# The first weight loads in order of use, another order of the first batch's Newton steps and M, idle products in slots 0 to 2

## The chip, the cores and the metric

One core of a Trainium2 chip runs the whole program. It has TensorE (PE, with its weight loads PEld), VectorE (DVE), ScalarE (ACT) and GpSimd (POOL) as engines that compute, SyncE (SP) as the queue that issues the transfers, and 16 DMA engines. The metric is the device time of one execution in microseconds. The inputs lie in the chip's memory, and all that is needed to prepare them counts.

## The reference

A Nyström attention with 32 landmarks, a six-step iteration for an inverse, and behind it two feed-forward networks:

```python
q_lm = q.reshape(B, H, 32, S // 32, D).mean(axis=3)      # B, H, S, D = 4, 8, 576, 64
k_lm = k.reshape(B, H, 32, S // 32, D).mean(axis=3)
A, Bm, C = sm(q, k_lm), sm(q_lm, k_lm), sm(q_lm, k)      # softmax of scaled scores
Z = Bm.T / (norm1(Bm) * norminf(Bm) + 1e-6)
for _ in range(6):
    Z = 2 * Z - Z @ Bm @ Z
x = heads_side_by_side(A @ Z @ C @ v)                    # 2304 x 512
h = x @ w_in;   x = (h * clip(h + 3, 0, 6) / 6) @ w_out  # 512 -> 2048 -> 512
h = x @ w_in2;  x = where(h > 0, h, exp(min(h, 0)) - 1) @ w_out2
```

The four weight matrices come as 64-bit floats and have to be converted on the chip; the tensors q, k and v are 32-bit.

## The kernel before

**Slots.** The first network runs in slots: a slot is one block of 128 of the 2048 hidden columns for half a batch (288 tokens). Its first products (`slot_a1`, lines 837 to 865: six products h<-atl/ath,nh/nl into a bank "h") multiply the attention's factors directly: n is M times the weight matrix (`attn_n`, 804 to 832), and at is the transposed softmax A (`attn_at`, 791 to 802). Then ACT and DVE form the activation (gf, g), and three slots later the second products (`slot_a2`, 867 to 886) add into four accumulators x. M itself (`finish`, 646 to 666) comes from the inverse Q and the values; Qd is Q spread over four heads, t0 the normalised values.

**The first part.** `start` (729 to 784) computes the first batch's attention up to the first slot. The order on PE, DVE, ACT and POOL is written out by hand in the string `PLAN` (723 to 727): each letter runs one step of a generator. b, c, a, v and B, C, A, V are the steps of the scores, the softmax of q and the values for the two head groups (a's and A's fifth step is the exponential on ACT, their sixth the sum, the reciprocal and a product on POOL); i is a step of `inverse` (586 to 644): three to set up, then for each of the six Newton iterations one step for PE's product and one for DVE's, and a last one that hands over Q; f is a step of `finish`; n makes the first 128 columns of n; t is `attn_at`, with three steps; x and y run the next conversion step of a weight unit on ACT or DVE; w is an idle product, 128x128 of the identity into a bank that nobody reads. PE works an idle product as two instructions, a product in 32-bit floats in general so.

**Weights.** A unit is one 128-column piece of a weight matrix, 512 KB of 64-bit floats. `steps` (211 to 241) loads it and then converts it with two passes on ACT, two on DVE and one addition on POOL. `units` holds four units of the first matrix (0 to 3), twelve of the second (l, l0 to l11), and four more of the first (m, m0 to m3). The digits, l and m in `PLAN` issue their loads. Slot by slot, `first_half` (1044 to 1088) converts one unit of each matrix, in the order 0, 1, 2, 3, then m0 with l0, m1 with l1 and so on. The tiles are named u, un or ub by their place.

**Queues.** All loads go through SP's queue. There the order isn't that of the program: the scheduler takes the instruction with the lowest `wanted` value first (`wanted`, 151). q and k have -70, unit 0 -66, v -65, unit 1 -64, the other eighteen all -50. On the four computing engines the program's order holds until slot 35 (`strict`); from slot 36 on the scheduler lays out their order, except where it is tied by hand. The second batch's attention is laced into slots 0 to 35 by the string `PLAN1` (1090); `newton` (675 to 715) does the third and fourth batch.

Of the kernel before, what the change touches and what calls it, by code (L numbers as in the profile page):

```python
# [10 lines left out]
F32 = mybir.dt.float32  # L11
# [20 lines left out]
def nystrom_ffn_kernel(ctx: ExitStack, tc, q, k, v, w_in1, w_out1, w_in2, w_out2, out):  # L32
# [32 lines left out]
    B, G, _, _, S = q.shape  # L65
# [58 lines left out]
    vec, act, pool, pe = InOrder(nc.vector), InOrder(nc.scalar), InOrder(nc.gpsimd), InOrder(nc.tensor)  # L124
# [15 lines left out]
    ident = const.tile([128, 128], F32, name="ident")  # L140
# [10 lines left out]
    def wanted(s):  # L151
        tc.cur_priority = int(1000 * (s + 100))
# [38 lines left out]
    banks, marks = {}, {}  # L191
# [51 lines left out]
    def run(gen):  # L243
        for _ in gen:
            pass
# [397 lines left out]
            yield 1.0  # L643
        return X[:, :, 2]

    def finish(b, Q, cvs, sc):

        t0 = ap_.tile([128, G, D], F32, name="t0", tag="t0")
        vec.scalar_tensor_tensor(
            out=sc[:, 0], in0=sc[:, 0], scalar=1e-9, in1=sc[:, 1], op0=ALU.add, op1=ALU.add  # L650
        )
        vec.reciprocal(out=sc[:, 0], in_=sc[:, 0])
        vec.tensor_tensor(out=t0, in0=cvs, in1=sc[:, 0].unsqueeze(2).to_broadcast([128, G, D]), op=ALU.mult)
        Qd = ap_.tile([128, G, 4, 32], F32, name="Qd", tag="Qd")
        vec.tensor_tensor(
            out=Qd, in0=Q.unsqueeze(2).to_broadcast([128, G, 4, 32]),
            in1=onesbd.rearrange("p (h j) -> p h j", h=4).unsqueeze(1).to_broadcast([128, G, 4, 32]), op=ALU.mult,
        )
        yield 1.0
        mps = bank()[:, 0:128]  # L660
        for g in range(G):
            amm(mps[64 * g:64 * g + 64, :], t0[:, g, :], Qd[:, g].rearrange("p h j -> p (h j)"), True, True)
        yield 0.5
        mt = ap_.tile([128, 4, 32], F32, name="mt", tag="mt", bufs=1)
        vec.tensor_copy(out=mt.rearrange("p a c -> p (a c)"), in_=mps)
        mt_t[b] = mt
# [8 lines left out]
    def newton(b):  # L675

        EB, sb, sc, cvs = newton_tiles()
        s = [SB * (b - 1) + (NEW if b > 1 else NEW1)]
        kept = {}

        def go(gen, n=99):
            for _ in range(n):
                wanted(s[0])
                try:
                    s[0] += next(gen) * (PACE if b > 1 else PACE1)
                except StopIteration:
                    return

        def keep(key, gen):
            kept[key] = yield from gen  # L690

        go(prep(b, 0))
        go(score_b(b, 0, sb, EB))
        go(keep(0, score_c(b, 0, sc)))
        go(soft(b, 0))
        go(values(b, 0, kept[0], cvs))
        go(prep(b, 1))
        go(score_b(b, 1, sb, EB))
        inv = keep("Q", inverse(EB, sb))
        sC = keep(1, score_c(b, 1, sc))  # L700
        sA = soft(b, 1)
        go(inv, 1)
        go(sC, 2)
        go(inv, 1)
        go(sC)
        go(inv, 2)
        go(sA, 3)
        go(inv, 2)
        v1 = values(b, 1, kept[1], cvs)
        go(v1, 2)  # L710
        go(inv, 2)
        go(sA)
        go(v1)
        go(inv)
        go(finish(b, kept["Q"], cvs, sc))

# [2 lines left out]


    PLAN = """
        0123llllmmmmllllllll kk b cc k bb k c B CC B c B c i i C xx v a i C v a C
        iwwavi iwwavVi vViwwAyVi aAiwwAVi VxxiwwAi aiwwyi
        ixAfwwwfwwwAfwwwtyywwwnwwwtwwxt
    """

    def start():

        EB, sb, sc, cvs = newton_tiles()
        kept = {}

        def keep(key, gen):
            kept[key] = yield from gen

        warm = bank()[:, 0:128]
        units = [[u, None] for u in conv_in1(0)]
        units += [[conv_out1(kk), None] for kk in range(NFILL)]
        units += [[u, None] for u in conv_in1(1)]  # L740

        def preps():
            for g in range(G):
                yield from prep(0, g)

        def fill(eng):

            for x in units:
                if x[1] and x[1][0] is eng:
                    x[1] = next(x[0], ())  # L750
                    while x[1] and x[1][0] is pool:
                        x[1] = next(x[0], ())
                    return

        make = {
            "k": preps, "f": lambda: finish(0, kept["Q"], cvs, sc), "n": lambda: attn_n(0, 0, 128),
            "i": lambda: keep("Q", inverse(EB, sb)), "t": lambda: attn_at(0, 0, vec),
        }
        for g in range(G):
            for name, gen in (  # L760
                ("b", lambda g=g: score_b(0, g, sb, EB)),
                ("c", lambda g=g: keep(g, score_c(0, g, sc))), ("a", lambda g=g: soft(0, g)),
                ("v", lambda g=g: values(0, g, kept[g], cvs)),
            ):
                make[name.upper() if g else name] = gen
        gens = {}
        for c in "".join(PLAN.split()):
            wanted(-60)
            if c in "xy":
                fill(act if c == "x" else vec)  # L770
            elif c == "w":
                pe.matmul(warm, lhsT=ident, rhs=ident, start=True, stop=True)
            elif c in "lm" or c.isdigit():
                wanted(-66 if c == "0" else -64 if c == "1" else -50)
                x = units[int(c)] if c.isdigit() else next(
                    x for x in (units[MPC:] if c == "l" else units[MPC + NFILL:]) if x[1] is None
                )
                x[1] = next(x[0], ())
            else:
                if c not in gens:  # L780
                    gens[c] = make[c]()
                next(gens[c], None)
        run(gens["t"])
        return units, gens["n"]
# [252 lines left out]
    def loads(b):  # L1037
        load_v(b, 0)
        for g in range(G):
            for what in "kq":  # L1040
                yield
                load_qk(b, g, what)

    def first_half(units, n0):

        outs = units[MPC:MPC + NFILL] + [[conv_out1(kk), None] for kk in range(NFILL, NKT)]
        groups = [units[0:2], units[2:4]]
        for j in range(NKT):
            group = [outs[j]]
            if MPC + j < NKT:  # L1050
                if j % MPC == 0:
                    ins = [[u, None] for u in conv_in1(j // MPC + 1)] if j else units[MPC + NFILL:]
                group.insert(0, ins[j % MPC])
            groups.append(group)
        ns, na = n0, 1
        sp.on = True
        for i in range(-PRE, NKT):
            between[0] = banks["h"].tile([128, 512], F32, name="h", tag="h")
            stream(groups, i + PRE + 1)
            wanted(i)  # L1060
            if i >= 0:
                run(slot_a1(i))
            while na < min(NKT, i + (NLEAD if 0 < i < MPC - 2 else 1) + 1):
                if na % MPC == 0:
                    run(ns)
                    ns = attn_n(0, na // MPC, 256)
                next(ns, None)
                na += 1 if na < MPC else 2
            if i >= DELAY:
                run(slot_a2(i - DELAY))  # L1070
            if i == NKT - 1:
                stream(groups, len(groups) + 3)
                between[0] = None
            if i < 0:
                continue
            if i >= GATE1:
                yield
        run(ns)
        for i in range(NKT, END):
            wanted(i)  # L1080
            a1, a2 = slot_a1(i), slot_a2(i - DELAY)
            next(a1)
            yield
            for dm in range(NDM):
                next(a1, None)
                next(a2, None)
                yield
            run(a2)

    PLAN1 = "ssssssuulslullslsssspppspsssppspppssssosssbbcsbsocsccscsaPasvaoavsssPvvosPavPasssPossPssPPssssssssBPoCCBssCCBososssisCsssisAississiAoAssissisVosiVAVVioiAsssAVisisisiioisssfftftssssotsnTssonssnosnsssnsnsTnosssnsssTssssssss"  # L1090

    def second_half(slots):

        EB, sb, sc, cvs = newton_tiles()
        kept = {}
# [4 lines left out]
        def parts():  # L1100
# [1 line left out]
                yield from attn_n(1, c, 256)  # L1102

        make = {
            "u": lambda: attn_at(0, 1), "o": splits, "l": lambda: loads(1), "f": lambda: finish(1, kept["Q"], cvs, sc), "n": parts,
            "i": lambda: keep("Q", inverse(EB, sb)), "t": lambda: attn_at(1, 0), "T": lambda: attn_at(1, 1),
        }
        for g in range(G):
# [6 lines left out]
        gens = {"s": slots}  # L1115
# [159 lines left out]
```

## Time and profile before

| what | value |
|---|---|
| median of 3 runs | 841.47 us (841.1 to 843.55) |
| the profiled execution's own time | 841.77 us |
| its span, first to last instruction | 840.0 us |
| PE busy | 795.5 us, 95% |
| PE weight loads busy | 697.0 us, 83% |
| DVE busy | 511.3 us, 61% |
| ACT busy | 445.7 us, 53% |
| POOL busy | 335.4 us, 40% |
| mean granted TensorE clock | 0.977 |
| moved by DMA | 165.63 MB |

Busy time is what the profiler records for one execution; a busy PE is not PE at its peak, since the ends of products are modelled. A row of the trace gives the start, the duration, the engine, the operation, what it writes and reads, how many instructions are merged in the row (x), and in brackets how long the engine was idle just before and what ended that. The idle time of an engine that isn't on the path to the end costs nothing. Nearly all instructions carry the line 110, that of the helper through which every one is issued, so they are told apart by their tiles.

### The profile page before, as it was taken

The page shows a single profiled execution, that of the slowest core. Times are in us where ns is not written, and L with a number is a line of the kernel's source. Part 1 is how long each engine was busy: PE and PEld are TensorE (multiplying, and loading weights), DVE is VectorE, ACT ScalarE, POOL GpSimd, SP SyncE. Part 2 cuts the span into 40 slices and gives each one's busy share as a digit, 9 for nine tenths or more (in the row PEclk, how much of TensorE's full clock was granted, in tenths as well). Part 3 has the DMA queues.
Part 4 walks back from the last instruction along what each step waited for, and adds up shares of the span by engine and source line. Part 5 has one row for each costly group of instructions (what it writes and reads, how often), then busy time and mean ns, then how long its engine had stood idle before and what let it go on. Part 6 is the DMA issues. An engine that isn't in the chain of part 4 may idle for free.

```text
span 840.0 us, 15410 instructions
## 1 busy us (share of the span) xinstructions
PE 795.5 (95%) x5650; PEld 697.0 (83%) x5650; DVE 511.3 (61%) x1026; ACT 445.7 (53%) x977; POOL 335.4 (40%) x348
## 2 busy tenths in 40 slices
PE   5669999999999999999999899999999999999998
PEld 4447778779888898979989789999989899999996
DVE  6488867647535565356585877656565545645544
ACT  3178654555646655576565565655544434534433
POOL 2256666636655545445656756431380000000000
PEclk9759999999999999999999999999999999999999
DMA  9935972386558433664482377586763564663531
GB/s 336 372 101 151 312 248 65 98 255 221 177 171 251 148 125 117 210 217 161 143 315 85 116 254 287 207 310 246 252 217 139 184 224 170 229 234 139 198 129 75
DMA packets 95563, 165.63 MB, mean 197 GB/s; under 512 B 7232, under 2 KB 51264, under 8 KB 95488
## 3 DMA queue, kind: packets, MB, share of 16 engines
q1 hardware_dynamic: 95488, 164.66, 57.9%
q8 instruction: 44, 0.72, 0.4%
q14 instruction: 31, 0.25, 0.1%
HBM read 119.54 MB, written 45.09 MB: 196 GB/s over the span
## 4 chain that ended last, share of the span: by engine, by line
PE 70%; DVE 6%; DMA 5%; POOL 3%; issue 3%; ACT 2%; SPq 1%; POOLq 0%; DVEq 0%; ACTq 0%
PE x L110 38%; PE h L110 27%; PE bk L110 4%; DVE u L110 2%; DMA u<-in_moe_w_in 1%; POOL x L110 1%; DMA w1c<-w1d 1%; DVE gf L110 1%; DMA u<-in_moe_w_out 1%; DVE gl L110 1%; DVE x L110 1%; ACT gf L110 1%; SPq L110 1%; POOL xf L110 1%; DMA x<-x1d 1%
## 5 line engine op out<-in xcount | busy, mean ns | idle before, releaser
L110 PE MATMUL h<-x,wi 128*128 128x384 f32 x1008 | 205.7, 339 | 0.8 <-DVE y L110 0.7
L110 PE MATMUL x<-gh,wo 128*128 128x288 f32 x896 | 201.4, 300 | 3.5 <-ACT xs L110 3.2
L110 PEld LDWEIGHTS h<-x,wi 128*128 128x128 f32 x1008 | 182.0, 189 | 15.2 <-DVE u L110 1.3
L110 PEld LDWEIGHTS x<-gh,wo 128*128 128x128 f32 x896 | 150.1, 189 | 13.1 <-issue 6.8
L110 PE MATMUL x<-gl,wo 128*128 128x288 f32 x448 | 132.2, 298 | 0.1
L110 ACT CAST gh<-gf 128x288 fp32r<-128x288 f32 (+1 forms) x172 | 78.9, 461 | 86.2 <-DVE gf L110 86.0
L110 POOL TENSOR_TENSOR gl<-gf,gh 128x288 fp32r<-128x288 f32 x100 | 83.8, 841 | 88.2 <-ACT gh L110 75.9
L110 PE MATMUL x<-w,gh 128*128 128x512 f32 x360 | 116.5, 394 | 1.1 <-ACT gh L110 1.1
L110 ACT ACTIVATE gf<-y 128x384 f32<-128x384 f32 x96 | 50.4, 525 | 101.4 <-DVE y L110 101.3
L110 DVE SCALAR_TENSOR_TENSOR gf<-gf,y 128x384 f32<-128x384 f32 x96 | 63.3, 660 | 57.1 <-ACT gf L110 57.1
L110 PE MATMUL h<-atl,nh 128*128 128x288 f32 x256 | 82.9, 324 | 9.3 <-DVE g L110 7.1
L110 PE MATMUL x<-w,ghl 128*128 128x512 f32 x324 | 89.2, 392 | 0.0
L110 PEld LDWEIGHTS x<-gl,wo 128*128 128x128 f32 x448 | 84.7, 189 | 3.0 <-issue 2.2
L110 ACT ACTIVATE gf<-h,half_b 128x288 f32<-128x288 f32 x128 | 64.0, 501 | 34.8 <-PE h L110 32.0
L110 DVE SCALAR_TENSOR_TENSOR gf<-gf,h 128x288 f32<-128x288 f32 x112 | 49.9, 447 | 47.9 <-ACT gf L110 47.6
L110 PE MATMUL h<-ath,nh 128*128 128x288 f32 x256 | 77.1, 301 | 0.0
L110 PE MATMUL h<-ath,nl 128*128 128x288 f32 x256 | 77.1, 301 | 0.0
L110 PEld LDWEIGHTS x<-w,gh 128*128 128x128 f32 x360 | 67.4, 189 | 10.6 <-ACT gh L110 1.5
L110 PE MATMUL x<-w,gl 128*128 128x512 f32 x180 | 71.2, 396 | 3.6 <-DVE gl L110 3.6
L110 PEld LDWEIGHTS h<-atl,nh 128*128 128x128 f32 x256 | 49.2, 192 | 24.1 <-issue 7.9
L110 PEld LDWEIGHTS x<-w,ghl 128*128 128x128 f32 x324 | 60.2, 188 | 8.4
L110 DVE TENSOR_TENSOR gl<-gf,gh 128x384 fp32r<-128x384 f32 (+1 forms) x72 | 48.2, 671 | 18.2 <-ACT gh L110 14.6
(148 smaller groups left out, 1271.2 us busy)
## 6 DMA issues: line engine op xcount, KB each, us to landing
wi<-wi2p SPq DMA_DIRECT2D x64, 448.0 KB, 5.0
w<-wo2p SPq DMA_DIRECT2D x32, 512.0 KB, 6.1
wi2p<-wi SPq DMA_DIRECT2D x32, 448.0 KB, 2.8
u<-in_moe_w_in SPq DMA_DIRECT2D x25, 512.0 KB, 4.6
w1c<-w1d SPq DMA_DIRECT2D x48, 256.0 KB, 4.7
ub<-in_moe_w_out SPq DMA_DIRECT2D x16, 512.0 KB, 10.2
u<-in_moe_w_out SPq DMA_DIRECT2D x16, 512.0 KB, 5.5
wo2p<-w SPq DMA_DIRECT2D x16, 512.0 KB, 3.2
```

Source lines behind the costliest of these rows:

```text
L110: inst = getattr(self.eng, name)(*a, **kw)
```

## The change

The change does three things. It gives each of the twenty first weight loads a `wanted` value of its own, from -66 for unit 0 and -63.5 for unit 1 up to -54.5, and lists l and m in turns. It writes another order for the first batch behind the common beginning of `PLAN`: the idle products between the Newton steps are gone (10 of 29 stay in the first part), the conversion steps of units 0 to 2 stand elsewhere, and `finish` has one more step, so that the normalised values t0 can be made before the last Newton step; it now takes Q when Qd is made. Since `finish` has four steps, `PLAN1` has one f more. And slots 0 to 2, which have no second products, get eight idle products each, behind the first products and n.

```diff
-    def finish(b, Q, cvs, sc):
+    def finish(b, kept, cvs, sc):
 
         t0 = ap_.tile([128, G, D], F32, name="t0", tag="t0")
...
         vec.reciprocal(out=sc[:, 0], in_=sc[:, 0])
         vec.tensor_tensor(out=t0, in0=cvs, in1=sc[:, 0].unsqueeze(2).to_broadcast([128, G, D]), op=ALU.mult)
+        yield 0.6
+        Q = kept["Q"]
         Qd = ap_.tile([128, G, 4, 32], F32, name="Qd", tag="Qd")
...
-        yield 1.0
+        yield 0.4
         mps = bank()[:, 0:128]
...
     PLAN = """
-        0123llllmmmmllllllll kk b cc k bb k c B CC B c B c i i C xx v a i C v a C
-        iwwavi iwwavVi vViwwAyVi aAiwwAVi VxxiwwAi aiwwyi
-        ixAfwwwfwwwAfwwwtyywwwnwwwtwwxt
+        0123lmlmlmlmllllllll kk b cc k bb k c B CC B c B c i i C xx v a i C v a C
+        iavi iavivV ViAyAi VyiaAi ViVAi xx iafi iAfwfwwfwwAtyywnwwtxxwwt
     """
...
-        gens = {}
+        gens, nth = {}, 0
         for c in "".join(PLAN.split()):
...
             elif c in "lm" or c.isdigit():
-                wanted(-66 if c == "0" else -64 if c == "1" else -50)
+                wanted(-66 if c == "0" else -64 + nth)
+                nth += 0.5
...
             if i >= DELAY:
                 run(slot_a2(i - DELAY))
+            elif i >= 0:
+                warm = banks["x"].tile([128, 512], F32, name="x", tag="x")[:, 0:128]
+                for _ in range(8):
+                    pe.matmul(warm, lhsT=ident, rhs=ident, start=True, stop=True)
...
-    PLAN1 = "...isisisiioisssfftftssssots..."
+    PLAN1 = "...isisisiioisssffftftssssots..."
```

The calls of `finish` hand over `kept` instead of `kept["Q"]`.

## Rows read from the trace of the kernel before

**Rows 1.** The page's 40 slices of 21 us, PE's busy tenths

```profile
PE   5669999999999999999999899999999999999998
```

**Rows 2.** Busy time by stage: stretch, length, engines (instructions), clock, DMA share, GB/s

```profile
0.00:43.00 43.00, 25.39 (x341) 18.93 (x341) 25.51 (x67) 11.98 (x31) 11.88 (x32) 0.88 0.92 345
43.00:66.00 23.00, 16.96 (x111) 11.96 (x111) 18.68 (x37) 18.05 (x39) 12.96 (x10) 0.56 0.37 102
66.00:104.00 38.00, 35.38 (x237) 26.15 (x235) 33.79 (x62) 28.18 (x57) 26.05 (x21) 1.00 0.79 240
...
350.00:500.00 150.00, 140.87 (x930) 132.30 (x931) 100.74 (x181) 92.21 (x204) 86.63 (x80) 0.98 0.55 186
```

**Rows 3.** ACT in order of time, around its longest wait: start, duration, operation

```profile
36.30 0.66 ACT L110 ACTIVATE w1c<-un 128x512 f32<-128x512 f32 x1 [10.62 <-DMA un<-in_moe_w_in]
36.87 0.67 ACT L110 ACTIVATE ea<-ea 128x576 f32<-128x576 f32 x1
```

**Rows 4.** DVE in order of time, from the values' normalising to M's copy

```profile
26.73 0.98 DVE L110 SCALAR_TENSOR_TENSOR sc<-sc 128x2 f32<-128x2 f32 x1
...
29.01 0.41 DVE L110 TENSOR_TENSOR Qd<-X,onesbd 128x256 f32<-128x256 f32 x1
37.57 0.75 DVE L110 TENSOR_REDUCE st<-ea 128x18 f32<-128x576 f32 x1 [8.15 <-ACT ea L110]
...
38.75 0.23 DVE L110 COPY mt<-bk 128x128 f32<-128x128 f32 x1
```

**Rows 5.** PE in order of time: last Newton product, idle products, M, idle products

```profile
25.19 0.33 PE L110 MATMUL bk<-X 32*32 32x32 f32 x16
25.45 1.38 PE L110 MATMUL bk<-ident 128*128 128x128 f32 x10
29.56 0.70 PE L110 MATMUL bk<-Qd,t 128*64 128x128 f32 x4 [2.74 <-DVE Qd L110]
...
39.73 2.50 PE L110 MATMUL bk<-ident 128*128 128x128 f32 x10
```

**Rows 6.** SP's issues of tile un, and the landing times of that tile's loads

```profile
7.39 0.35 SPq L110 DMA_DIRECT2D un<-in_moe_w_in  x1
...
26.09 0.33 SPq L110 DMA_DIRECT2D un<-in_moe_w_in  x1
...
DMA to landing us min/median/max: 9.6/10.6/11.6
```

**Rows 7.** POOL beside the values' normalising

```profile
26.29 1.41 POOL L110 TENSOR_TENSOR ea<-ea,st 128x576 f32<-128x576 f32 x1 [0.89 <-DVE st L110]
```

**Rows 8.** PE, first products of slots 0, 1, 3, and slot 0's second products

```profile
42.96 0.58 PE L110 MATMUL h<-atl,nh 128*128 128x288 f32 x1 [0.73 <-DVE atl L110]
...
48.09 0.58 PE L110 MATMUL h<-atl,nh 128*128 128x288 f32 x1 [2.18 <-DVE g L110]
...
56.66 0.61 PE L110 MATMUL h<-atl,nh 128*128 128x288 f32 x1 [2.32 <-DVE g L110]
...
59.44 4.09 PE L110 MATMUL x<-g,ub 128*128 128x288 f32 x8
```

**Rows 9.** PE, slot 1's second products, and slot 9's first

```profile
64.16 2.10 PE L110 MATMUL x<-g,ub 128*128 128x288 f32 x8
...
80.15 0.40 PE L110 MATMUL h<-atl,nh 128*128 128x288 f32 x1 [1.16 <-DVE g L110]
```

**Rows 10.** Busy time and granted clock (the number behind POOL) of short stretches

```profile
12.00:14.00 2.00, 1.19 (x12) 0.56 (x8) 1.79 (x11) 1.69 (x7) 0.00 (x0) 1.00 1.05 281
...
16.00:24.00 8.00, 8.00 (x190) 5.67 (x190) 5.15 (x13) 3.09 (x9) 1.16 (x1) 1.00 1.03 408
...
29.00:30.00 1.00, 0.44 (x4) 0.33 (x4) 0.42 (x2) 0.00 (x0) 0.00 (x0) 0.57 1.05 418
...
32.00:33.00 1.00, 1.00 (x9) 1.00 (x8) 0.00 (x0) 0.00 (x0) 0.00 (x0) 0.72 0.98 389
...
43.00:62.00 19.00, 12.96 (x93) 8.68 (x94) 16.07 (x32) 15.93 (x35) 10.37 (x8) 0.50 0.37 112
```

More of the change, by code (lines that the diff above doesn't have):

```diff
@@ L714, in newton @@
         go(inv)
-        go(finish(b, kept["Q"], cvs, sc))
+        go(finish(b, kept, cvs, sc))
     PLAN = """
-        0123llllmmmmllllllll kk b cc k bb k c B CC B c B c i i C xx v a i C v a C
-        iwwavi iwwavVi vViwwAyVi aAiwwAVi VxxiwwAi aiwwyi
-        ixAfwwwfwwwAfwwwtyywwwnwwwtwwxt
+        0123lmlmlmlmllllllll kk b cc k bb k c B CC B c B c i i C xx v a i C v a C
+        iavi iavivV ViAyAi VyiaAi ViVAi xx iafi iAfwfwwfwwAtyywnwwtxxwwt
     """
@@ L755, in start @@
         make = {
-            "k": preps, "f": lambda: finish(0, kept["Q"], cvs, sc), "n": lambda: attn_n(0, 0, 128),
+            "k": preps, "f": lambda: finish(0, kept, cvs, sc), "n": lambda: attn_n(0, 0, 128),
             "i": lambda: keep("Q", inverse(EB, sb)), "t": lambda: attn_at(0, 0, vec),
@@ L1088, in first_half @@
             run(a2)
-    PLAN1 = "ssssssuulslullslsssspppspsssppspppssssosssbbcsbsocsccscsaPasvaoavsssPvvosPavPasssPossPssPPssssssssBPoCCBssCCBososssisCsssisAississiAoAssissisVosiVAVVioiAsssAVisisisiioisssfftftssssotsnTssonssnosnsssnsnsTnosssnsssTssssssss"
+    PLAN1 = "ssssssuulslullslsssspppspsssppspppssssosssbbcsbsocsccscsaPasvaoavsssPvvosPavPasssPossPssPPssssssssBPoCCBssCCBososssisCsssisAississiAoAssissisVosiVAVVioiAsssAVisisisiioisssffftftssssotsnTssonssnosnsssnsnsTnosssnsssTssssssss"
     def second_half(slots):
@@ L1104, in second_half @@
         make = {
-            "u": lambda: attn_at(0, 1), "o": splits, "l": lambda: loads(1), "f": lambda: finish(1, kept["Q"], cvs, sc), "n": parts,
+            "u": lambda: attn_at(0, 1), "o": splits, "l": lambda: loads(1), "f": lambda: finish(1, kept, cvs, sc), "n": parts,
             "i": lambda: keep("Q", inverse(EB, sb)), "t": lambda: attn_at(1, 0), "T": lambda: attn_at(1, 1),
```

## The prediction

> **What bounds the kernel now.** I read the page's slices first [rows 1]: TensorE (PE) is busy nine tenths or more of nearly every slice, but not of the first three, of 21 us each. The table of stages [rows 2] sizes that: from 0 to 43 us PE works 25.4 us and DMA is near its limit; from 43 to 66 us PE works 17.0 of 23, at a mean granted clock of 0.56; from 66 to 104 PE is fairly full, but DVE with 33.8 of 38 us is what the slots wait for. Behind that only 350 to 500 us has idle PE to speak of, 9.1 us. So a front that ends sooner moves the end by as much, unless something behind it is due at a fixed time.
>
> Then the hole in DVE and ACT [rows 3, 4]. ACT waits 10.62 us, from 25.68 on, for one load, unit 2's (tile un), and the exponential of the second head group, queued behind it, starts only at 36.87, though it needs nothing of unit 2. DVE has written Qd by 29.42 and stands 8.15 us until that exponential is there; behind it in DVE's order is the copy of M (38.75), though PE had M's products at about 30.3 [rows 4, 5]. M feeds n, and n feeds the first slot. The load is late by its place, not by rate: SP issued it, by the landing time, at 26.09, behind ten loads of the second matrix that the first slots don't need yet, and a load lands 9.6 to 11.6 us after its issue in this stretch [rows 6]; 26.09 plus 10.2 is 36.3, when ACT goes on.
>
> **The loads in the order of use.** Twenty loads of 512 KB stay twenty; only their places in SP's queue differ. Unit 2 takes the first un place, issued at 7.39, and lands at 17 to 19 us; unit 3 and then l0, m0, l1, m1 follow, one each 1.34 us (fourteen issues from 7.39 to 26.09 [rows 6]), so m1 is there by 26 and l11 by 41 as now. ACT wants m0 and l0 some 2 us into slot 0, m1 and l1 about 3 us later, so no slot below waits for a load, and l4 to l11, which lose places, aren't needed before slot 4. The stores of w1d and the next u loads behind them keep their place on SP. Price nil; its cover is some 8 us of lead, and were that gone each load would cost its spacing, 1.34 us.
>
> **The plan of the first batch.** The change also moves unit 2's two ACT passes behind the exponential and behind n's casts, so the wait leaves the path even without the new load order. What is late next is the Newton chain. In its stretch PE is never idle now (its second row in [rows 10]), and five pairs of idle products lie between its first and last product; five products took 1.38 us at the full clock [rows 5], so ten are 2.8. If all of it came off, the last Newton product would start at 22.4 instead of 25.19; if DVE's answers bind, at 25.19 as now. Each Newton step on DVE must first see its product, and transposes and one conversion share DVE's order; following the new order through I get 23.4, nearer the first end.
>
> DVE then: sum of exponentials, its scalar and its reciprocal, 1.2 us (the same three ran from 37.57 to 38.75 [rows 4]), so done at 24.5 if they start at 23.3. The normalising of the values now stands here, ahead of the last Newton step. Its first operation, on two columns, took 0.98 us and ended at 27.71 with POOL's 1.41 us product (27.70) [rows 4, 7]; I take that stall again, since the same POOL product starts at the same moment: 24.5 + 1.41 + about 0.5 for the reciprocal and t0 is 26.4. Last Newton step 0.2 and Qd 0.41: 27.0. M's products start 0.14 behind Qd and their copy 0.6 later: 27.75, with 0.23 for itself 28.0. The sum of the second exponentials starts there instead of at 37.57. From that row to slot 0's first product are 5.4 us now (37.57 to 42.96 [rows 4, 8]), the same DVE steps in the same order. Slot 0 starts at about 33.4: **9.6 us sooner**. Without POOL's stall it is 11.2; with no Newton gain at all 7.8.
>
> The nine idle products that PE now gets between M's products and slot 0 take 0.28 us each at the full clock and 0.50 at the low one (five took 1.38 and 2.50 [rows 5]): 2.5 to 4.5 us, beside 5.4 us of DVE work in which PE has only n's products, about 0.7 us, to do besides. Hidden, just so at the low clock.
>
> **Idle products in slots 0 to 2.** Eight each, 2.2 us at the full clock, 4.0 at the low one. The cover is PE's idle time ahead of the next slot's products [rows 8]: 2.18 us ahead of slot 1, none that has a row ahead of slot 2, 2.32 ahead of slot 3. At the full clock slots 0 and 2 are covered. In slot 1 PE is late by 2.2 at most and by nothing at least, since ACT and DVE are queued with conversions there; the slot's own products take half the time at the full clock, which gives back a part, and I take 0.2. What they buy: the eight second products of slot 0 ran 4.09 us at the low clock, 2.10 for the same eight a slot later [rows 8, 9]. PE is 2.0 us sooner at slot 4, but later slots wait for DVE (1.16 us ahead of slot 9 [rows 9]), and DVE has only its idle time of 43 to 66 us, 4.3 in all [rows 2], of which I count the third that lies at PE's late slot 4: 1.4 less 0.2 is **1.2 us sooner**.
>
> Whether the clock is up there: it fell between 29 and 30, behind PE's pause of 2.74 us ahead of M [rows 5]; it came back between 32 and 33, PE working from 29.56 on; and from 43 to 62 it stayed at 0.50 (1.2 GHz) though PE was busy two thirds of the time [rows 10]. In the new plan PE pauses about 2 us ahead of M, then works nearly through into slot 0 for over 5 us. So I take it as up (2.4 GHz) in slot 0, and keep the other case below.
>
> The Trainium skill ("TensorE: Matmul & The Clock Gate", Part 1) says that the throttled state is the default and that activity releases it. That speaks against taking 19 of 29 idle products out of the first part; by it the Newton stretch could run at 1.2 GHz, which is rival A with its own price. The trace agrees with the rule where PE stood still, and no row shows the Newton stretch without idle products.
>
> **The rest.** finish in two steps: in the second batch's plan the four f stand together, same order, nil; for batches 2 and 3 Qd is due a fraction of a slot sooner or later, at most its own 0.41 us twice [rows 4]: plus or minus 0.8, taken as nil. From slot 36 on the scheduler orders ACT, DVE, POOL and SP itself, and a moved front can lay that out anew: with 9.1 us of PE idle to be shifted [rows 2] I take nil and plus or minus 2.
>
> **Sum.** 840.0 less 9.6 less 1.2 is a span of 829.2; with the 1.77 us around it (841.77 was this execution) 831.0; the median of the runs lies 0.3 under this execution: **830.7 us**, bounds of its own 827.5 to 834.
>
> **Rivals.**
> A. The Newton stretch falls to 1.2 GHz. PE was busy 8.0 us there with some 2.8 of idle products [rows 10, 5], so about 5 to 7 us of work would take up to twice the time, partly beside DVE: 5 us lost, 835.7. Against it: at 12 to 14 us, 60% busy, the clock stayed full [rows 10]. 0.08.
> B. The clock stays at 0.50 in slots 0 to 2. Eight products are 4.0 us each: 1.8 too long in slot 0, about 3 in slot 1, 1.7 in slot 2, and the 1.2 us aren't won: 7.7 lost less some cover, 837. For it: the clock stayed low there before [rows 10]. 0.12.
> C. The change doesn't do what it says: SP's order isn't the listed one, and unit 2 still lands at 36.3. ACT then stands behind n's casts, and the second half of slot 0's operand waits to about 38.5: 4.5 us won instead of 9.6, 836. Against it: each load now has a priority of its own. 0.05.
> D. Slower. The place is the change from the first network to the second, 350 to 500 us, where PE is already idle 9.1 us [rows 2]. If the scheduler puts the conversions of the second network's weights behind the activations there, PE's idle time must grow by over 10.8 us, more than double, before the gain is gone; at 13.5 us the time is 844. Against it: what is moved lies 300 us ahead. 0.05.
>
> **How the numbers follow.** My case 0.66, A 0.08, B 0.12, C 0.05, D 0.05; 0.04 for a gain beyond 827.5. A measurement of this kernel can tell 0.3%, 2.5 us, from no change: all but D and a little of B and C are faster by more. Faster 0.91, same 0.04, slower 0.05. The range takes in my own bounds and A, B and C: 827.5 to 837.0.
>
> **What would show it.** ACT's wait for un is gone and the un loads stand among the first issues. The second sum of exponentials on DVE starts near 28, slot 0's first product near 33.4 (31.5 to 35.5). The granted clock is 1.00 from slot 0 or 1 on, and slot 0's second products take 2.1 us, not 4.1. The time from slot 4 on is as long as before within 2 us. I am wrong if slot 0 starts after 36, if slot 0's second products start later behind slot 0's first than now (59.44 less 42.96, 16.5 us), or if the time from there on grows.

## The result and the profile after

| what | before | changed |
|---|---|---|
| median, runs of one comparison | 842.12 us | 831.97 us (831.52 to 835.77) |
| profiled execution's own time, span | 841.77, 840.0 us | 832.15, 830.4 us |
| PE, DVE busy | 795.5, 511.3 us | 791.3, 509.3 us |
| mean granted TensorE clock | 0.977 | 0.987 |

The changed kernel is faster: the ratio is 0.9888, its 95% interval 0.9855 to 0.9921. A later comparison of the same two gave 833.09 against 842.6 us, 0.9899 (0.9865 to 0.9933). Forecast were 830.7 us and a span of 829.2. Ratios below are of fast runs alone; one execution of the run with the plan alone took 1527.77 us and stands outside its ratio.

The stages, which answer to [rows 2 and 10]: stretch, length, busy time of PE, its weight loads, DVE, ACT and POOL with instructions in brackets, granted clock, DMA share, GB/s.

```profile
0.00:43.00 43.00, 28.86 (x380) 21.05 (x381) 32.85 (x82) 19.60 (x49) 16.87 (x36) 0.84 0.99 368
43.00:66.00 23.00, 22.20 (x165) 17.57 (x165) 21.91 (x40) 19.65 (x40) 15.62 (x12) 1.00 0.57 158
...
350.00:500.00 150.00, 139.14 (x889) 131.34 (x890) 101.61 (x182) 90.87 (x201) 90.17 (x81) 0.98 0.55 190
...
26.00:28.00 2.00, 1.08 (x6) 0.78 (x7) 1.08 (x5) 0.00 (x0) 0.04 (x1) 0.58 1.05 412
28.00:30.00 2.00, 2.00 (x13) 1.77 (x12) 1.93 (x5) 0.00 (x0) 0.74 (x1) 0.50 1.02 401
...
38.00:40.00 2.00, 2.00 (x12) 2.00 (x11) 1.93 (x6) 2.00 (x5) 0.74 (x1) 0.50 1.03 381
40.00:42.00 2.00, 1.19 (x22) 0.76 (x21) 1.93 (x4) 1.15 (x4) 1.75 (x2) 1.00 1.09 387
```

Between 43 and 66 us PE is now busy 22.2 of 23 us at the full clock, where it was busy 17.0 at a mean of 0.56; these are later slots than before, and most of two groups of idle products lies in them. The last four lines hold a surprise: the clock fell at about 26.3 us and stayed low to 40, over slot 0.

SP's issues of the changed kernel in order of time, which answer to [rows 6]:

```profile
7.49 1.76 SPq L110 DMA_DIRECT2D un<-in_moe_w_in  x2
...
11.60 0.33 SPq L110 DMA_DIRECT2D un<-in_moe_w_in  x1
...
19.73 8.00 SPq L110 DMA_DIRECT2D ub<-in_moe_w_out  x6
```

Units 2 and 3 are issued first, then the second and the first matrix in turns. ACT no longer waits for un anywhere in the first part. DVE and POOL, which answer to [rows 4 and 7]:

```profile
24.65 0.10 DVE L110 SCALAR_TENSOR_TENSOR sc<-sc 128x2 f32<-128x2 f32 x1
24.80 0.17 DVE L110 RECIPROCAL sc<-sc 128x2 f32<-128x2 f32 x1
25.48 0.71 DVE L110 TENSOR_TENSOR t<-cvs,sc 128x128 f32<-128x128 f32 x1 [0.51 <-DVE sc L110]
...
26.35 0.43 DVE L110 TENSOR_TENSOR Qd<-X,onesbd 128x256 f32<-128x256 f32 x1
27.65 0.29 DVE L110 COPY mt<-bk 128x128 f32<-128x128 f32 x1 [0.88 <-PE bk L110]
27.86 0.74 DVE L110 TENSOR_REDUCE st<-ea 128x18 f32<-128x576 f32 x1
...
24.88 1.16 POOL L110 TENSOR_TENSOR ea<-ea,st 128x576 f32<-128x576 f32 x1 [0.86 <-ACT ea L110]
```

And PE from the last Newton product to slot 0's second products, which answers to [rows 5, 8 and 9] (an idle product is two instructions, so x16 are eight; those into x are the slots'):

```profile
23.62 0.33 PE L110 MATMUL bk<-X 32*32 32x32 f32 x16 [0.41 <-DVE X L110]
...
26.92 0.70 PE L110 MATMUL bk<-Qd,t 128*64 128x128 f32 x4 [2.56 <-DVE Qd L110]
27.55 2.50 PE L110 MATMUL bk<-ident 128*128 128x128 f32 x10
...
30.59 2.08 PE L110 MATMUL bk<-ident 128*128 128x128 f32 x8
33.26 0.58 PE L110 MATMUL h<-atl,nh 128*128 128x288 f32 x1 [0.60 <-DVE atl L110]
...
36.14 3.78 PE L110 MATMUL x<-ident 128*128 128x128 f32 x16
39.58 0.56 PE L110 MATMUL h<-atl,nh 128*128 128x288 f32 x1
...
42.24 0.55 PE L110 MATMUL bk<-w1c,mt 64*32 64x128 f32 x16 [1.05 <-DVE nl L110]
42.73 2.05 PE L110 MATMUL x<-ident 128*128 128x128 f32 x16
44.54 0.38 PE L110 MATMUL h<-atl,nh 128*128 128x288 f32 x1
...
48.66 2.21 PE L110 MATMUL x<-g,ub 128*128 128x288 f32 x8
50.49 0.51 PE L110 MATMUL h<-atl,nh 128*128 128x288 f32 x1
```

Slot 0 starts at 33.26 instead of 42.96 us, 9.70 sooner; slot 4 at 50.49 instead of 63.03, 12.54 sooner; the activation of slot 16 on ACT at 93.2 instead of 105.0, 11.78 sooner. That stands to slot 80 (11.4) and slot 92 (340.7 against 353.5, 12.8); by slot 116 it is 9.0, and at the end 9.6.

### The profile page after: what moved, and what is told of

Its sections match the earlier page's. It is cut to its first block, busy times and chain, and to the rows that moved or that the text cites. A ratio compares the mean times of both kernels' runs of the same rounds, so it can differ in the third digit from the quotient of the medians.

```text
span 830.4 us, 15433 instructions
## 1 busy us (share of the span) xinstructions
PE 791.3 (95%) x5660; PEld 696.1 (84%) x5660; DVE 509.3 (61%) x1026; ACT 445.7 (54%) x977; POOL 335.1 (40%) x348
## 4 chain that ended last, share of the span: by engine, by line
PE 62%; DMA 8%; DVE 8%; issue 5%; POOL 4%; ACT 3%; SPq 1%; POOLq 0%; ACTq 0%; DVEq 0%
PE x L110 34%; PE h L110 25%; PE bk L110 4%; DMA u<-in_moe_w_out 2%; DMA x<-x1d 2%; DVE u L110 1%; DMA u<-in_moe_w_in 1%; DVE x L110 1%; DVE y L110 1%; DVE gf L110 1%; POOL x L110 1%; DMA out<-ob 1%; POOL y L110 1%; ACT gf L110 1%; DVE gl L110 1%
## 5 line engine op out<-in xcount | busy, mean ns | idle before, releaser
L110 PEld LDWEIGHTS x<-w,ghl 128*128 128x128 f32 x324 | 60.2, 188 | 8.4
```

The source lines that it names most:

```text
L110: inst = getattr(self.eng, name)(*a, **kw)
```

## How the runs are read

Two executions of one and the same kernel differ in the front (last section): DVE's first sum of exponentials (st<-ea) starts anywhere from 17.2 to 19.8 us. So I count the steps from that sum on. In the table, all in us from one profiled execution each, "sum" is the start of that first sum, "slot 0" the time from it to slot 0's first product, "to 4" from there to slot 4's first product, "to 16" from slot 0's first product to slot 16's activation; the median is of all the runs of that kernel.

| kernel | sum | slot 0 | to 4 | to 16 | median |
|---|---|---|---|---|---|
| before | 17.22 | 25.74 | 20.07 | 62.1 | 842.1 |
| changed | 17.32 | 15.94 | 17.23 | 60.0 | 832.0 |
| the same, later | 19.39 | 16.38 | 17.33 | 60.3 | 833.1 |
| loads only | 19.75 | 19.00 | 19.37 | 61.3 | 834.1 |
| plan only | 18.55 | 16.33 | 23.43 | 66.5 | 840.5 |
| slot products only | 17.23 | 25.83 | 17.35 | 60.2 | 841.7 |
| loads and plan | 19.53 | 16.77 | 18.72 | 61.6 | 835.2 |
| loads and slot products | 19.67 | 18.99 | 18.43 | 61.2 | 835.5 |
| products in the Newton steps | 17.27 | 17.02 | 17.12 | 60.1 | 833.3 |
| pause ahead of M filled | 19.69 | 18.00 | 17.11 | 60.1 | 831.9 |
| products at the start | 19.56 | 16.78 | 17.25 | 60.3 | 835.0 |
| products from the start on | 17.73 | 16.79 | 18.73 | 61.5 | 832.6 |
| no products in slot 0 | 19.10 | 16.34 | 18.96 | 61.7 | 834.2 |
| pause in slot 1 filled | 17.64 | 16.45 | 16.88 | 60.1 | 831.2 |

My theory after the result: the order of the loads and the plan of the first batch together give slot 0's 9.7 us, and the idle products in the slots give some 2 us more by bringing the clock up sooner. The rivals: one of the first two is enough alone; the slot products only fill idle time; the Newton steps lose by running without idle products.

## The experiments

**The changed kernel once more**, beside the others.

> The changed kernel once more, as it is. What it tells apart: in its first trace the start of slot 92 came 12.8 us sooner than before, slot 116 only 9.0, and the end 9.6, though the order of instructions on every engine is the same as before from slot 3 on. My theory (the stretch from 340 to 430 us wanders by itself, with transfers that land sooner or later): the gain at slots 64, 92 and 116 differs from the first trace by 1 us or more while the end stays within 1.5. Rival (the moved front costs 2 us there, every time): the same 12.5, 12.8 and 9.0 within 0.5.

833.09 us (832.01 to 836.11), 0.9899 (0.9865 to 0.9933). Its profiled execution has the first sum 2.07 us later than the first one of the same kernel, and slot 0 2.51 later; from there on it is the same within 0.4 us to slot 16. In the stretch from slot 92 to slot 116 the two profiles differ as well, by 1.5 us (below). So one execution's front is known to no better than 2 us, and differences of medians below that say little without the trace.

**The order of the loads alone.** The kernel before, with

```diff
-        0123llllmmmmllllllll kk b ...
+        0123lmlmlmlmllllllll kk b ...
...
-                wanted(-66 if c == "0" else -64 if c == "1" else -50)
+                wanted(-66 if c == "0" else -64 + nth)
+                nth += 0.5
```

> The kernel before with the new order of the twenty loads alone (same plan, no idle products in slots). My theory (the late unit 2 held the path; its place in SP's queue is enough to free it): ACT's 10.62 us wait for un is gone, the second sum of exponentials on DVE starts right behind Qd, near 29.5 instead of 37.57, but n waits behind the nine idle products after M (to about 33.6), so slot 0 starts at 35 to 36.5: 6.5 to 8 us won of the 9.7, 834 to 835.5 in all. Rival (the order of loads is the whole change): slot 0 at 33.3 and 832. Rival (the wait is hidden by something else that is as late): less than 2 us won.

834.07 us, 0.9911 (0.9881 to 0.9941). Slot 0 stands 19.00 us behind the first sum instead of 25.74: 6.7 of the 9.8 us that the whole change wins there. The first slots go much as before, mostly at the low clock (19.37 us to slot 4). Slot 16's activation stands 80.3 us behind the first sum, where it stood 87.8 before and stands 75.9 and 76.7 in the two profiles of the changed kernel. So most of the gain needs only the load order; the order of the first batch isn't needed to end ACT's wait.

**The plan alone.** The changed kernel with the old load order and without the slot products (the diff above the other way round, and the block of slot products taken out).

> The changed kernel with the old order of loads and without the idle products in slots: the new plan alone. My theory: unit 2 still lands at about 36.3, now behind n's casts and the first half of slot 0's operand on ACT; M and n come as early as in the changed kernel (M's copy near 27.7), slot 0's first three products start near 33.3, but the second three wait for ACT, to about 38.5, so slot 1 and what follows are some 4 us later than in the changed kernel, and slot 4 another 2.8 without the products: 4 to 6 us won against the kernel before, 836 to 838. Rival (the plan is the change, the load order redundant): slot 1 within 1 us of the changed kernel, 833 to 834. Rival (the load is the change): no gain, 841 to 842.

840.49 us, 0.9963 (0.9947 to 0.998). The first line is ACT, the others PE, in order of time:

```profile
36.30 0.66 ACT L110 ACTIVATE w1c<-un 128x512 f32<-128x512 f32 x1 [3.15 <-DMA un<-in_moe_w_in]
...
34.88 0.37 PE L110 MATMUL h<-atl,nh 128*128 128x288 f32 x1 [0.59 <-DVE atl L110]
...
38.37 0.61 PE L110 MATMUL h<-atl,nh 128*128 128x288 f32 x1 [2.86 <-DVE atl L110]
...
54.72 3.99 PE L110 MATMUL x<-g,ub 128*128 128x288 f32 x8
```

This is rival C's case of the prediction. Unit 2 lands at 36.30 as before, ACT waits 3.15 us for it, and the second half of slot 0's operand comes at 38.37 where rival C said about 38.5. So slot 1 starts 8.48 us behind slot 0 instead of 5.13, and that is all that makes the 23.43 us to slot 4 longer than the 20.07 before: the slots run at the low clock in both. Rival C's time of 836 was for the rest of the change staying. The plan alone is worth 1.8 us by the medians and 3.1 by the ratio, less than the 4 to 6 us expected, though slot 0's first half starts as early as in the changed kernel. By the landmark it is worth more: slot 16's activation stands 82.9 us behind the first sum instead of 87.8. Of these 4.9 us this execution lost 1.3 ahead of the first sum and 2.3 behind slot 16.

**Loads and plan, without the slot products.**

```diff
-            elif i >= 0:
-                warm = banks["x"].tile([128, 512], F32, name="x", tag="x")[:, 0:128]
-                for _ in range(8):
-                    pe.matmul(warm, lhsT=ident, rhs=ident, start=True, stop=True)
```

> The changed kernel without the 24 idle products in slots 0 to 2. My theory (they buy the clock back, and slot 4 with it): slot 0 as in the changed kernel (33.3), granted clock 0.50 until slot 3 or 4, slot 4's first product at about 53.3 instead of 50.5, of which DVE gives back 0.8 by slot 8: 2 us slower than the changed kernel in the slots, 833.5 to 834.5 in all. Rival (DVE binds the slots, so PE's clock is worth nothing there): slot 16 within 0.5 us of the changed kernel's 92.0, 832.

835.21 us, 0.9914 (0.9888 to 0.994). One stretch of its table of stages, over slots 2 and 3:

```profile
48.00:52.00 4.00, 2.04 (x14) 1.69 (x22) 3.83 (x8) 3.51 (x8) 3.23 (x3) 0.50 0.00 0
```

Without the products the clock is still 0.50 there, and slot 16 is 61.6 us behind slot 0 instead of 60.0 and 60.3. By the clock changes that the trace files keep, the last rise of the front comes 17.4 us behind slot 0's start here and 20.3 in the kernel before, but 6.7 and 6.9 in the two profiles of the changed kernel: the products bring the clock up earlier. They are worth 1.3 to 1.6 us at slot 16.

**The slot products alone**, in the kernel before.

> The kernel before with the 24 idle products in slots 0 to 2 alone. My theory: slot 0 starts where it did (43.0), the clock is back by slot 1, slot 4 comes 2 to 2.8 us sooner than 63.03, slot 16 about 2 us sooner than 103.82: 839 to 840.5. Rival (nothing or a loss: PE is held up by products at the low clock, and DVE binds anyway): slot 16 within 0.5 us of 103.82 or later, 841 to 843.

841.72 us, 0.9994 (0.9983 to 1.0006). The trace has the gain: slot 4 stands 17.35 us behind slot 0 instead of 20.07, and slot 16's activation is 1.73 us sooner than before. But the execution's span is only 1.2 us shorter, and over the runs less than 1.5 us shows. By medians this part is not to be told from nothing; by its place in the trace it is 1.7 us.

**Idle products put back between the Newton steps** of the changed kernel, five pairs (the expectation counts four).

```diff
-        iavi iavivV ViAyAi VyiaAi ViVAi xx iafi ...
+        iwwavi iwwavivV ViwwAyAi VyiwwaAi ViwwVAi xx iafi ...
```

> The changed kernel with the pairs of idle products between the Newton steps put back (four pairs, after the products of the first four of the six steps). My theory (PE binds the Newton chain, each pair costs its 0.55 to 0.64 us there): from the first sum of exponentials on DVE to the last Newton product 7.3 to 8.4 us instead of 6.3, slot 0 later by as much, 833 to 834. Rival (the products pay for themselves by keeping the clock up into slot 0): slot 0 no later, the clock at 1.00 in slot 0, 832 or less. Rival (DVE binds the chain): within 0.3 us of 6.3.

833.34 us, 0.9899 (0.9872 to 0.9925). The last Newton product stands 7.81 us behind the first sum instead of 6.30 and 6.75 in the two profiles of the changed kernel, and slot 0 17.02 instead of 15.94 and 16.38. So in these executions the products cost 1.1 to 1.5 us on the chain there and 0.6 to 1.1 by slot 0; the medians (833.34 and 833.09) don't tell the kernels apart. They buy nothing for the Newton steps: without them a group of sixteen products bk<-X takes 0.42 to 0.43 us as in the kernel before, so rival A of the prediction (the Newton steps at 1.2 GHz) didn't come in the first profile of the changed kernel. In the second only the first group was slower, at 0.49 us; with the pause ahead of M filled (below) the clock fell ahead of the last two groups, which took 0.65 and 0.44 us instead of 0.43 and 0.33.

**The pause ahead of M filled**, eight idle products behind the last Newton product, so that PE wouldn't stand still there.

```diff
-        ... ViVAi xx iafi iAfwfww ...
+        ... ViVAi xx iwwwwwwwwafi iAfwfww ...
```

> The changed kernel with eight more idle products behind the last Newton product, where PE now pauses 2.56 us ahead of M and behind which the clock falls. My theory (the pause is why slot 0 runs at the low clock, against my prediction): the granted clock stays at 1.00 through slot 0, slot 0's eight products take 2.2 instead of 3.78 us, slot 1 starts 5.1 instead of 6.3 us after slot 0, slot 4 about 1 us sooner, slot 16 by 0.5 to 1 us: 831 to 831.5. Rival (the clock falls all the same, since the PE share around it is too low): clock 0.50 in slot 0 and no change, 832. Rival (M is held up by the products): slot 0 later, 832.5 or more.

831.89 us, 0.9891 (0.9863 to 0.9919). PE in order of time:

```profile
25.56 0.33 PE L110 MATMUL bk<-kqv,ect 96*32 96x64 f32 x9 [1.33 <-issue]
...
27.22 4.21 PE L110 MATMUL bk<-ident 128*128 128x128 f32 x18
31.36 0.70 PE L110 MATMUL bk<-Qd,t 128*64 128x128 f32 x4
```

The clock fell all the same in this execution, behind an earlier pause of 1.33 us, so the products ran at 0.47 us each and held M until 31.36, though DVE had Qd ready at 30.00; slot 0 is 18.00 us behind the first sum, 1.6 to 2.1 later than without. The median doesn't show it. The run says that a pause filled with idle products turns into a delay when the clock falls ahead of it; whether the products hold the clock where it is up isn't answered by it.

**Nine idle products at the start**, at 1.70 to 5.81 us, to bring the clock up before the score products.

```diff
-        0123lmlmlmlmllllllll kk b ...
+        wwwwwwwww 0123lmlmlmlmllllllll kk b ...
```

> The changed kernel with nine idle products ahead of all else on PE, from about 2 to 7 us, where PE waits for the first transfer. Why: up to the first sum of exponentials on DVE the traces need 17.3 us (before, changed, products alone) or 18.6 to 19.8 (the three others), and in the late ones the score products take 2.19 instead of 1.19 us up to 18 us. My theory (PE starts at the low clock, and when it rises is left to chance): with the products the first sum comes at 16.5 to 17.2, and the slow starts are gone: 830.5 to 831.5, with less spread. Rival (the late starts come from transfers): no change, 832, the first sum between 17.3 and 19.8 as before.

834.99 us, 0.9917 (0.9894 to 0.994). PE:

```profile
7.92 1.16 PE L110 MATMUL bk<-kt,bd 128*64 128x288 f32 x7
...
16.52 2.19 PE L110 MATMUL bk<-qt,bd 128*64 128x288 f32 x8
```

The first score products were fast, the later ones slow again, and the first sum was at 19.56: the clock came up and fell again before it was needed. The median lies above both forecasts.

**Loads and slot products with the old plan**, to see what the plan adds.

> The old order of the first batch with the new load order and the 24 slot products: the changed kernel without its second part. If the three parts add up, it is the load order alone (834.1) less the 1.7 us that the slot products won at slot 16 without it: 832.4, slot 0 some 19 us behind DVE's first sum as with the load order alone, slot 16's activation 78.6 us behind that sum, where the whole change has 75.9; the order of the first batch is then worth 2 to 3 us on top. Rival: once loads and slot products are there, the new order adds nothing by slot 16, since DVE binds from slot 4 on: 76 behind the first sum and a median as the changed kernel's, 832.0 or less.

835.45 us, 0.9915 (0.9885 to 0.9945): 3 us more than expected of either. Slot 0 is 18.99 us behind the first sum, as with the loads only, so by the traces the new plan is worth 2.6 to 3.1 us at slot 0 on top of the load order; the medians don't settle it. The miss is in the slots (61.2 to slot 16, as without any slot products). PE:

```profile
40.89 2.05 PE L110 MATMUL x<-ident 128*128 128x128 f32 x16
...
47.54 0.78 PE L110 MATMUL bk<-w1c,mt 64*32 64x128 f32 x16 [2.33 <-DVE nl L110]
48.25 3.13 PE L110 MATMUL x<-ident 128*128 128x128 f32 x16
```

The clock was up in slot 0 and fell in slot 1, at a pause of 2.33 us in which PE waits for DVE between the slot's two pieces of n. Slot 1's eight products then took 3.13 us, and slot 2 started 7.33 us behind slot 1 instead of 4.96.

**Products from the start on**: the changed kernel with 14 idle products first and eleven between the score products (the expectation counts nine).

```diff
-        0123lmlmlmlmllllllll kk b cc k bb k c B CC ...
+        0123lmlmlmlmllllllll wwwwwwwwwwwwww kk wwww b wwww cc www k bb k c B CC ...
```

> The changed kernel with 14 idle products ahead of the first product and nine more between the first score products, so that PE never stands long in the first 12 us. If PE's clock, rising at about 12 us in some executions and at 19 in others, is what makes DVE's first sum of exponentials start at 17.3 or at 18.6 to 19.8, and steady work raises it at the same time in each execution, then the first sum starts at 16.8 to 17.3, the first eight products qt,bd take 1.19 us and not 2.19, and the times lie at 831 to 831.8 within 1 us of each other. Rival: the time of the rise is not PE's doing, and the products only hold up the score products: first sum at 19 to 20.5 and 834 to 836.

832.64 us (831.3 to 834.09), 0.9888 (0.9865 to 0.9911). PE:

```profile
15.57 1.19 PE L110 MATMUL bk<-qt,bd 128*64 128x288 f32 x8
...
43.36 0.55 PE L110 MATMUL bk<-w1c,mt 64*32 64x128 f32 x16 [1.76 <-DVE nl L110]
43.84 3.68 PE L110 MATMUL x<-ident 128*128 128x128 f32 x16
```

The score products are fast from the first on and the first sum comes at 17.73, 0.4 later than expected for an early rise. But the times aren't closer together than 2.8 us, so the start isn't the only thing that varies. The other is in the last two lines: again the clock fell in slot 1 behind the pause (1.76 us), and slot 2 came 7.34 us behind slot 1.

**No products in slot 0** of the changed kernel, only in slots 1 and 2.

```diff
-            elif i >= 0:
+            elif i >= 1:
```

> The changed kernel without slot 0's eight idle products, which ran at the low clock (3.78 us) and behind which slot 1 started 6.32 us after slot 0 instead of 5.13. If they are what brings the clock up, as it rose at 40 us right behind them, then without them it stays 0.50 beyond 45 us, slot 0's second products take over 3 us and slot 16's activation stands 77.5 to 78.4 us behind the first sum (78.4 without any slot products): about 833.5. Rival: they only hold up slot 1; it then starts about 1.2 us sooner, the clock comes up in slot 1 or 2 all the same, and slot 16 stands at 75 to 76 behind the first sum: 831 to 832.

834.18 us (831.2 to 837.53), 0.9903 (0.987 to 0.9936). PE:

```profile
40.53 0.58 PE L110 MATMUL h<-atl,nh 128*128 128x288 f32 x1 [2.79 <-DVE g L110]
...
44.98 3.70 PE L110 MATMUL x<-ident 128*128 128x128 f32 x16
```

Slot 1 now starts 5.09 us behind slot 0, not 6.32: the eight products of slot 0 at the low clock do cost it 1.2 us, as the rival had it. But PE stands still 2.79 us instead, the clock stays low over slot 1, whose products take 3.70 us, and slot 16 is 61.7 us behind slot 0. So by this execution those eight pay for themselves by the clock that they bring to slots 1 and 2; the times of the runs, from 831.2 to 837.53, don't settle it.

**The pause in slot 1 filled**: the kernel with products from the start on, and of slot 1's eight idle products now ten, six of them between its two pieces of n.

```diff
             while na < min(NKT, i + (NLEAD if 0 < i < MPC - 2 else 1) + 1):
+                if i == 1 and pieces:
+                    idle(6)
+                pieces += 1
...
             elif i >= 0:
+                idle(4 if i == 1 else 8)
```

> The changed kernel with idle products from its start, as one run before, and of slot 1's eight now six between its two pieces of n, where PE paused 1.05 to 1.76 us for DVE, and four behind. If that pause is what let the clock fall in slot 1 (0.50 there and slot 1's eight products 3.68 us, against 2.05 where it stayed up), then the ten products run at 0.25 us each, slot 2's first product starts 11.3 us behind slot 0's as in the changed kernel and not 12.7, slot 16's activation stands 59.9 to 60.4 us behind slot 0's first product and not 61.5, and the median is 831.0 to 831.6. Rival: the fall in slot 1 doesn't hang on that pause; the products then take 4 to 5 us, slot 16 stands at 61.5 or more behind slot 0, and the median is 832.5 or more.

831.2 us (830.8 to 832.32), 0.9863 (0.9846 to 0.9881), the lowest median of all and the closest runs. PE:

```profile
36.31 2.05 PE L110 MATMUL x<-ident 128*128 128x128 f32 x16
...
40.57 1.60 PE L110 MATMUL x<-ident 128*128 128x128 f32 x12
42.96 0.55 PE L110 MATMUL bk<-w1c,mt 64*32 64x128 f32 x16 [0.79 <-DVE nl L110]
...
44.36 0.38 PE L110 MATMUL h<-atl,nh 128*128 128x288 f32 x1
```

The pause is 0.79 us, the clock stays up, slot 4 stands 16.88 us behind slot 0 and slot 16 60.1. Slot 2 starts 10.27 us behind slot 0, sooner than the 11.3 expected, since here the clock was up over slot 0 too (2.05 us). That the fall in slot 1 comes from the pause there is supported by this run and by two above, with pauses of 2.33 and 1.76 us; but it is one execution each, and not every such pause brings the clock down: the changed kernel kept it through 1.05 us, and the one with the pause ahead of M filled through 1.86. The edit also gives slot 1 two more products, and no run tells the place of the products from their number. The interval overlaps the changed kernel's, so that this version is faster than it is likely, not settled.

## Why the prediction was right, and where it was wrong

**Right, by their own steps.** The load order at price nil: units stand in SP's queue as listed, no slot waits for one of the twenty loads, and this part alone moves slot 0 by 6.7 us. The last Newton product: 23.4 forecast, 23.62 measured. Second sum of exponentials: 28.0 forecast, 27.86. Slot 0: 33.4 forecast, 33.26, 9.70 us sooner for 9.6. Part of this closeness is luck: in the second profile the last Newton product stands 0.45 us later behind the first sum, and slot 0 0.44. The nine idle products ahead of slot 0: hidden "just so at the low clock"; they ran at the low clock (2.50 and 2.08 us) and PE still waited 0.60 us for DVE's atl behind them. finish in two steps: nil; between slots 16 and 80 the gain stays at 11.8, within 0.7 us. The medians, 832.0 and 833.1, lie in the range of 827.5 to 837.0.

**Right sum, wrong place: the values' normalising.** I took POOL's stall at the two-column operation again, "since the same POOL product starts at the same moment". It wasn't there: the operation took 0.10 us, not 0.98, as it began at 24.65, ahead of POOL's 24.88. The Trainium skill ("SBUF — State Buffer", Who interferes with whom) says that a DVE operation with two inputs in SBUF contends with a GpSimd operation that reads SBUF, and that the order of issue decides who waits. Both traces agree: before, the operation began at 26.73 inside POOL's product (26.29 to 27.70) and ended with it. The reciprocal and t0, for which I allowed 0.5 us, took 1.39 (24.80 to 26.19), with a wait of 0.51 ahead of t0 that stands in the trace of before too, at 0.52. And t0, with two inputs, began inside the same POOL product and ended 0.15 us behind its end (26.04). It ended 0.15 us behind another product of POOL in the trace of before (29.08, 28.93), and 0.14 to 0.15 behind one in every other profile here. The rows of before, DVE and POOL:

```profile
28.43 0.65 DVE L110 TENSOR_TENSOR t<-cvs,sc 128x128 f32<-128x128 f32 x1 [0.52 <-DVE sc L110]
27.66 1.27 POOL L110 TENSOR_TENSOR w1c<-w1c,u 128x512 uint32<-128x512 uint32 x1
```

So the stall was there, at t0 instead of two operations earlier, and POOL's product sets when t0 is done: 26.19 where I had 26.4. How long t0 takes beside an idle POOL no run shows.

**Wrong: the clock in slot 0.** "So I take it as up (2.4 GHz) in slot 0": in both profiled executions of the changed kernel it was 0.50 there. Slot 0's eight products took 3.78 us and pushed slot 1 from 5.13 to 6.32 us behind slot 0, which is rival B's mechanism in its first slot. From 40 us on the clock was up, and B's other slots didn't come. It can come out the other way: with the pause in slot 1 filled, and with loads and slot products only, the same eight products of slot 0 took 2.05 us. I treated as one answer what is one of two.

**Wrong size: the slots' term.** 1.2 us forecast; 2.84 won by slot 4, 2.1 left from slot 9 on. I priced one thing, slot 0's second products (4.09 to 2.21 us; forecast 2.1), and cut it to the third of DVE's idle time that lies at slot 4. In fact slots 0 and 1 became longer by 1.2 and 0.5 us, and from slot 2 to slot 4 all of PE's products ran at the full clock, 5.95 us instead of 10.49. DVE gave back 0.8 of it by slot 9, so the step "later slots wait for DVE" held and the cover was larger than the third that I counted.

**Right only by its bounds: what comes behind.** I let the scheduler from slot 36 on lay out its order anew, nil and plus or minus 2. It did not: the order of instructions on every engine is the same as before behind the first slots. Still 2.2 us were given back between slot 16 and the end. A sign that I had named went against me with it: from slot 4 on the time should be as before within 2 us, and it is 779.9 us instead of 777.0 (779.3 in the second profile). Of these 2.9 us DVE's give-back up to slot 9 is 0.8. The stretches from slot 92's activation to slot 116's, and from there to the end; before:

```profile
353.50:418.90 65.40, 62.24 (x467) 59.24 (x466) 37.60 (x71) 42.31 (x97) 37.25 (x39) 0.97 0.56 179
418.90:840.00 421.10, 410.49 (x2098) 370.69 (x2097) 252.53 (x458) 206.79 (x423) 109.81 (x90) 0.99 0.57 201
```

and changed:

```profile
340.70:409.95 69.25, 62.10 (x461) 58.64 (x461) 37.45 (x71) 42.43 (x97) 37.52 (x39) 0.98 0.52 171
409.95:830.40 420.45, 411.02 (x2110) 372.36 (x2108) 251.37 (x458) 206.56 (x423) 109.65 (x90) 0.99 0.57 201
```

Much the same work on PE, but idle 7.15 us in the first stretch instead of 3.16. It overlaps rival D's place; over all of that, 350 to 500 us, PE's idle time went from 9.1 to 10.9 us and didn't double. In other executions with the same order the same stretch gave back less: 2.4 us in the second profile of the changed kernel, 0.6 with the pause in slot 1 filled. So it isn't a new order; it varies from execution to execution, and the chain runs through the conversion's transfers there (6.17 us of x<-x1d in one piece, 4.57 before). What decides its size was not tried and stays open.

**The sum.** 9.6 and 1.2 forecast; 9.7 and 2.1 measured, less 2.2 behind slot 16: a span of 830.4 instead of 829.2. The direction and the largest term rest on the load order, and there the reading of one wait [rows 3] and one queue [rows 6] was enough. The clock, on which I spent most words, moved 1 to 2 us.

## What to carry to other kernels

Look for an engine that waits long for one load with work queued behind it that doesn't need that load: putting the loads into the order of their use gave 0.9 of the 1.1 per cent here by itself, and the plan that moved the work past the wait gave 0.2 to 0.4 by itself. Idle products inside a pause went with a clock that stayed up in the one run that put them into slot 1, and held up M in the run where the clock had fallen ahead of them; at the low clock they take nearly twice as long (eight took 3.78 us instead of 2.05) and hold up the work that follows, so count them at that length. Compare kernels by a landmark behind the noisy start before a difference of 2 us is believed.

## What the runs showed of the hardware that I had not expected

**The clock's first rise comes at different times, and the stretch ahead of it reads as full clock.** The same eight products in two executions of the changed kernel, the first profile and the later one:

```profile
15.18 1.19 PE L110 MATMUL bk<-qt,bd 128*64 128x288 f32 x8
```

```profile
16.49 2.19 PE L110 MATMUL bk<-qt,bd 128*64 128x288 f32 x8
```

In the kernels without idle products at the start the durations change from the long to the short ones at about 12.5 us in some executions, with the first sum at 17.2 to 17.3, and at 17 to 20 in others, with the first sum at 18.6 to 19.8. What sets the time no run shows. The granted clock reads 1.00 in both from 12 to 18 us:

```profile
12.00:18.00 6.00, 5.71 (x39) 3.30 (x36) 4.46 (x23) 3.86 (x12) 0.00 (x0) 1.00 1.03 334
```

That is the later one, whose products took 2.19 us. The clock changes that the trace files keep begin with this very rise, at 12.7 us in the first profile and at 18.8 in the later one, and fit the durations; ahead of the first of them the view prints 1.00. I used a row of this kind [rows 10] as proof of a full clock, and it held only since the first recorded rise of the kernel before, at 12.1 us, stands at the start of that row; until its first recorded change the clock has to be read from the products' durations. The Trainium skill ("TensorE: Matmul & The Clock Gate", Part 1) warns that trn2's clock events in a profile have been seen to be unreliable and should be cross-checked. Here the recorded changes hold against the durations, and only the stretch ahead of the first of them misleads.

**PE stands still without a named releaser** between 21 and 26 us, while the DMA engines are busy throughout: 0.40 us in the first profile of the changed kernel and 1.12 in the second, 0.95 with products from the start on, 1.07 without products in slot 0, 1.33 with the pause filled, each in the midst of one group of products (kqv,ect) and marked as issue. It lies on the chain to M: the last Newton product stands 6.30, 6.75, 6.95, 6.70 and 7.16 us behind the first sum in these five. Its cause was not tried.
